# Four PSUM banks instead of three for the first MoE product, one of them freed by sharing; the first turn of keys in two instructions; one piece more per query unit

## The chip, the cores and the metric

The kernel runs on one core of a Trainium2 chip. The metric is the device time of one execution in microseconds. The engines are named as in the profile: PE is TensorE, DVE is VectorE, ACT is ScalarE, POOL is GpSimd, SP is SyncE, which here only issues DMAs. PEld is PE's loading of weights.

## The reference

Polysketch attention (4 batches, 4 heads, 1088 tokens, head dimension 32, sketch rank 8) is followed by a mixture of four experts with soft gates.

```python
a = einsum('rd,bhsd->bhsr', S1, x);  b = einsum('rd,bhsd->bhsr', S2, x)
phi(x) = outer(a, b) per token                       # 64 features
kv = einsum('bhsf,bhsd->bhfd', phi(k), v);  z = phi(k).sum(s)
attn = (phi(q) @ kv) / (phi(q) @ z + 1e-6)           # (B,H,S,D)
x = attn.transpose(0, 2, 1, 3).reshape(4352, 128)
p = domain_probs / (domain_probs.sum(-1) + 1e-9)     # (4352, 4)
out = sum_e p[:, e] * (relu(x @ w1[e]) @ w2[e])      # w1[e]: 128x1024, w2[e]: 1024x128
```

All is float32.

## The kernel before, in words

**The MoE is the backbone.** The 4352 tokens are cut into eleven chunks (`CHUNKS`: 128, 448, 512 six times, 320, 256, 128 columns). A chunk takes sixteen steps, one for each 256 of the 4096 hidden units. `first(i)` (line 744) makes two h tiles: for each it takes a PSUM bank with `psum(ps_h, "h")`, PE multiplies w1 by the transposed attention output `xT` into it, ACT writes the rectified half to `hid` (line 784), and DVE makes the sums and differences that a Strassen-like scheme wants (line 755). `second(i)` (line 798) is the product with w2, of seven block products instead of eight, which adds up in the two banks o0 and o1 over four steps. It runs for the step two earlier (`LA = 2`). At the end of an expert ACT copies o0 and o1 out (lines 889, 890) and POOL combines them (`gather`, `gather_rest`).

**Attention is cut into pieces.** The generator `front()` yields pieces of the next batch's keys and of the next query units; a unit is 128 to 512 tokens. `work()` is called after each h tile, so twice in a step, and calls `piece()` as often as a planner's credit allows. The planner adds up how many pieces must be done before each chunk can start (`needed`: 17 pieces for a batch's keys, 19 for a query unit, 21 for the first one), and spreads them evenly. A bare `yield` is an empty piece: it does no work and moves what follows to a later h tile. In each half step the program's order is: the h tile, then DVE's work on it, then the pieces. Every engine keeps its own part of this order.

**Keys** (`keys(b)`, line 423): three pieces turn the keys on DVE (`key_turn`, line 317; tiles 0 to 3, 4 to 7 and the last half tile), three project them on PE by the sketch matrix (`key_project_wide`, 4, 4 and 1 token tiles). ACT copies half of each projection from PSUM to SBUF (line 370), and DVE adds the other half to it (`key_add`, line 377). The add for group 0 is issued in the piece that projects group 1. Eight pieces form the 64 products by token and feature on DVE (`kp`, line 382), two pieces sum them against the values on PE (`key_sum`, into a bank of tag f), and one masks the result (`key_blocks`).

**Query units** (`queries`, line 608): turn the queries on DVE, project them on PE into f, shuffle and add on DVE, and form four products `qp` on DVE (line 485). After two empty yields comes `attend` (line 527): PE multiplies `qp` by the key sums into the bank `den` (three token tiles in a bank; a fourth goes to `num`), and DVE divides, turns and sends the result through DRAM into `xT`.

**PSUM** has eight banks of 512 float32 columns: three of tag h, o0, o1, f, den and num. A tag's bank is reused in turn, and the tile framework makes the new writer wait for the old tile's last reader.

**The start** (`start()`, line 653) does batch 0's keys and its first 128 queries at once, because PE has nothing else to do before the first `xT`: DVE turns keys (line 319) as soon as they land, PE projects them into three h banks and the queries into o0, o1 and num, DVE and POOL form products, PE sums them, and `attend_first` divides into `xT`. Three bf16 matmuls of zeros (`keep_warm`) run while PE waits.

Of the kernel before, what the change touches and what calls it, by code (L numbers as in the profile page):

```python
# [16 lines left out]
def _ap(t, p0: int, np_: int, off: int, free):  # L17

    p = list(t.ap)[0]
    return bass.AP(t.tensor, t.offset + p0 * p[0] + off, [[p[0], np_]] + [list(d) for d in free])  # L20
# [3 lines left out]
def kernel(  # L24
# [25 lines left out]
    P = 128  # L50
    HP = 64
    B, H, S, D = q.shape
# [20 lines left out]
    lpool = ctx.enter_context(tc.tile_pool(name="loads", bufs=1))  # L73
    apool = ctx.enter_context(tc.tile_pool(name="attn", bufs=1))
    mpool = ctx.enter_context(tc.tile_pool(name="moe", bufs=2))
    ps_h = ctx.enter_context(tc.tile_pool(name="ps_h", bufs=3, space=bass.MemoryType.PSUM))
    ps_o = ctx.enter_context(tc.tile_pool(name="ps_o", bufs=1, space=bass.MemoryType.PSUM))
    ps_f = ctx.enter_context(tc.tile_pool(name="ps_f", bufs=1, space=bass.MemoryType.PSUM))
    ps_n = ctx.enter_context(tc.tile_pool(name="ps_n", bufs=1, space=bass.MemoryType.PSUM))
# [3 lines left out]
    def psum(pool, tag):  # L83
        return pool.tile([P, 512], F32, tag=tag, name=tag)
# [25 lines left out]
    kn, qn, vn = {}, {}, {}  # L110
# [50 lines left out]
    kT = cpool.tile([P, P * NT], F32, name="kT")  # L161
# [152 lines left out]
    FG = ((0, 4), (4, 4), (8, 1))  # L314
    fss, kps, kvzs, kvx = {}, {}, {}, {}

    def key_turn(b, r):
        if r < 2:
            nc.vector.transpose(
                _ap(kT, 0, P, 512 * r, [[P, 4], [32, 4], [1, 32]]),  # L320
                _ap(kn[b], 0, P, P * r, [[32, 4], [8 * D, 4], [1, 32]]),
            )
        else:
            nc.vector.transpose(kT[:, 1024:S], kn[b][:, 1024:S])
# [98 lines left out]
    def keys(b):  # L423
        for r in range(3):
            key_turn(b, r)
            yield
        kf = []
        for gi, (pool, tag) in enumerate(((ps_f, "f"), (ps_n, "den"), (ps_n, "num"))):
            kf.append(psum(pool, tag))
            key_project_wide(b, gi, kf[gi])  # L430
            if gi:
                key_add(b, gi - 1, kf[gi - 1])
            yield
        for _ in value_copy(b):
            pass
        for t0, n in ((0, 4), (4, 5)):
            if t0:
                key_add(b, 2, kf[2])
            for p in range(2):
                for x in range(2):  # L440
                    key_product(b, t0, n, p, x, nc.vector)
                    yield
        kv = psum(ps_f, "f")
        for p in range(2):
            key_sum(b, p, kv)
            yield
        key_blocks(b, kv)
        yield
# [42 lines left out]

    def attend_first(b, c, n, qp):

        nd = [psum(ps_n, "den"), psum(ps_n, "num")]
        for _ in range(2):
            on_side(
                lambda s: nd[0][half[s], 0:n],
                lambda s: _ap(vx, 0, P, D, [[0, HP]]),
                lambda s: _ap(eps, 0, P, 0, [[0, n]]),
                start=True,  # L500
                stop=False,
            )
        for i in range(2):
            for _ in range(2):
                on_side(
                    lambda s: nd[i][half[s], 0:n],
                    lambda s: kvzs[b][:, s, 1 - i, :],
                    lambda s: qp[s][:, 0:n],
                    start=(i > 0),
                    stop=True,  # L510
                )
        yield

        rc = apool.tile([P, 2, HP], F32, tag="rd", name="rd")
        for i in range(2):
            by_g = [[32, 4], [1, 16]]
            nc.vector.reciprocal(_ap(rc, 0, P, HP * i, [[16, 4], [1, 16]]), _ap(nd[0], 0, P, 16 * i, by_g))  # L517
            nc.vector.tensor_tensor(
                out=_ap(xT, 0, P, HP * i, [[1, 4], [4, 16]]),
                in0=_ap(nd[1], 0, P, 16 * i, by_g),  # L520
                in1=_ap(rc, 0, P, HP * i, [[16, 4], [1, 16]]),
                op=ALU.mult,
            )
        have[0] += n
        yield

    def attend(b, c, n, qp):

        nd = [psum(ps_n, "den"), psum(ps_n, "num")]
        W = H * (D + 1)
        tiles = 0
        laid = []
        for c0, m in unit_parts(b, c, n):
            T = blocks(m)
            for p in range(2):
                for t in range(T[0]):
                    for _ in range(2):  # L540

                        at = c0 + P * t + (HP * turn[0] if t < T[turn[0]] else 0)
                        i, k = divmod(tiles + t, 3)
                        on_side(
                            lambda s: nd[i][half[s], W * k + W // 2 * p : W * k + W // 2 * (p + 1)],
                            lambda s: qp[p][:, at : at + HP],
                            lambda s: kvx[b][:, p, :],
                            start=True,
                            stop=True,
                        )  # L550
            laid.append((c0, T, tiles))
            tiles += T[0]
        yield
        banks = [(i, 3 * i, min(tiles, 3 * i + 3)) for i in range((tiles + 2) // 3)]
        rc = apool.tile([P, QW // 32], F32, tag="rc", name="rc")
        for i, t0, t1 in banks:
            nc.vector.tensor_scalar(
                out=rc[:, H * t0 : H * t1],
                in0=_ap(nd[i], 0, P, D, [[D + 1, H * (t1 - t0)]]),
                scalar1=1e-6, scalar2=1.0, op0=ALU.add, op1=ALU.mult,  # L560
            )
        nc.vector.reciprocal(rc[:, 0 : H * tiles], rc[:, 0 : H * tiles])
        yield
        xs = apool.tile([P, QW], F32, tag="qa", name="xs")
        for i, t0, t1 in banks:
            nc.vector.tensor_tensor(
                out=_ap(xs, 0, P, P * t0, [[D, H * (t1 - t0)], [1, D]]),
                in0=_ap(nd[i], 0, P, 0, [[D + 1, H * (t1 - t0)], [1, D]]),
                in1=_ap(rc, 0, P, H * t0, [[1, H * (t1 - t0)], [0, D]]),
                op=ALU.mult,  # L570
            )
        yield
        y = apool.tile([P, QW], F32, tag="y", name="y")
        for c0, T, t0 in laid:
            nc.vector.transpose(
                _ap(y, 0, P, P * t0, [[32, T[0]], [32 * T[0], H], [1, 32]]),
                _ap(xs, 0, P, P * t0, [[P, T[0]], [D, H], [1, D]]),
            )
            if b == 0 and c == P:
                for x in range(2):  # L580
                    yield
                    for a in (x, x + 2):
                        run = 32 * T[a // 2]
                        for h in range(H):
                            copy = nc.scalar.copy if h % 2 else nc.gpsimd.tensor_copy
                            at = S * b + c + a // 2 * 64 * T[0] + a % 2 * run
                            copy(xT[32 * h : 32 * h + 32, at : at + run], _ap(y, 32 * a, 32, 32 * T[0] * h, [[1, run]]))
                continue
            m = 64 * sum(T)
            base = xd.offset + P * (S * b + c + c0)  # L590
            for a in range(4):
                run = 32 * T[a // 2]
                nc.sync.dma_start(
                    bass.AP(
                        xd.tensor,
                        base + a // 2 * 64 * T[0] + a % 2 * run,
                        [[m, 32], [32 * m, H], [1, run]],
                    ),
                    _ap(y, 32 * a, 32, P * t0, [[32 * T[0], H], [1, run]]),
                )  # L600
            nc.sync.dma_start(
                xT[:, S * b + c + c0 : S * b + c + c0 + m],
                bass.AP(xd.tensor, base, [[m, P], [1, m]]),
            )
        have[0] += n
        yield

    def queries(b, c, n):
# [22 lines left out]
                yield  # L631
        yield
        yield
        yield from attend(b, c, n, qp)


# [16 lines left out]
    def start():  # L653
# [1 line left out]

        b, n = 0, UNITS[0][0]
        kf = []
        for r in range(3):
            key_turn(b, r)
        qT = query_turn(b, 0, n)  # L660
        for gi in range(3):
# [5 lines left out]
        key_project(b, 2, kf[2])  # L667
        for _ in value:
            pass
        fq = [psum(ps_o, "o0"), psum(ps_o, "o1"), psum(ps_n, "num")]  # L670
        for i in range(3):
            for j in range(2):
                both(fq[i][:, 0:n], sr[:, i, j, :], qT[:, 0:n], start=(j == 0), stop=(j == 1))
# [259 lines left out]
    for b in range(B):  # L933
        count += 17 if b else 0
        for n in UNITS[b] if b else UNITS[0][1:]:
            count, columns = count + (19 if count else 21), columns + n
            for m in range(NC):
                if columns - n < START[m] + CHUNKS[m] <= columns:
                    needed[m] = count
# [73 lines left out]
```

## Time and profile before

| | |
|---|---|
| median of 4 runs | 489.74 us (489.64 to 490.47) |
| the profiled execution | 489.55 us, of which the trace spans 487.6 us |
| PE busy | 481.7 us (99% of the span), 4545 matmuls |
| DVE busy | 323.5 us (66%) |
| ACT busy | 246.7 us (51%) |
| POOL busy | 228.3 us (47%) |
| granted TensorE clock | 1.0 |
| first MoE matmul | 13.58 us after the start of the span |

Times inside the trace count from the start of the span. A line of the groups gives the source line, engine and operation, the tiles out<-in, the shape and the number of instructions, then busy time and the mean of one in ns, and behind the second bar the engine's idle time just before them and what ended it. A PE row is a whole matmul with its latency, and several run at once, so PE's rate is read from the distance between starts. A float32 matmul shows as two rows. Line 193 is the helper that issues nearly all of them, so tile names tell them apart.

### The profile page before, as it was taken

Reading aid. Unit: us, or ns where it says so; the run is one execution under the profiler, and the core shown is the slowest. Engines: PE = TensorE matmul, PEld = TensorE weight load, DVE = VectorE, ACT = ScalarE, POOL = GpSimd, SP = SyncE. Lnnn points to the kernel's source line nnn. Section 1 sums busy time; section 2 is a strip of 40 time slices with the busy share of each in tenths; the row PEclk is TensorE's granted clock in tenths of the full one; section 3 lists DMA queues with packets and bytes.
Section 4 is the critical chain, followed back from the end, with each engine's and each line's share of the span. In section 5 each row is a group of like instructions: output and inputs, shape, how many; then the busy total and the mean of one; then the engine's idle time right before and its main releaser. Section 6 shows DMA issues by size and latency. Waiting matters only on the chain.

```text
span 487.6 us, 11352 instructions
## 1 busy us (share of the span) xinstructions
PE 481.7 (99%) x4545; PEld 359.7 (74%) x4545; DVE 323.5 (66%) x754; ACT 246.7 (51%) x496; POOL 228.3 (47%) x269
## 2 busy tenths in 40 slices
PE   8999999999999999999999999999999999999997
PEld 5877777677777777555777777777777777878997
DVE  6858685868776857768675676575575566655642
ACT  4364554445454635445455554545455455566751
POOL 6072563516345445324555353434555345555570
PEclk9999999999999999999999999999999999999999
DMA  7990230130103510041102200021101200120000
GB/s 209 290 301 6 85 98 1 32 107 1 35 1 109 126 40 1 1 118 24 34 1 86 50 2 2 1 86 24 34 0 56 50 1 0 50 51 3 15 3 18
DMA packets 37590, 26.25 MB, mean 54 GB/s; under 512 B 26018, under 2 KB 34594, under 8 KB 37026
## 3 DMA queue, kind: packets, MB, share of 16 engines
q1 hardware_dynamic: 37520, 25.53, 18.9%
q8 instruction: 36, 0.59, 0.5%
q14 instruction: 18, 0.13, 0.1%
q10 hardware_dynamic: 16, 0.00, 0.0%
HBM read 21.28 MB, written 4.24 MB: 52 GB/s over the span
## 4 chain that ended last, share of the span: by engine, by line
PE 96%; DVE 2%; issue 0%; DMA 0%; POOL 0%; ACT 0%; DVEq 0%
PE h L193 49%; PE o L193 40%; PE f L193 4%; PE den L193 2%; DVE qp L485 1%; DVE hid L755 1%; DMA s_raw<-in_S_dram 0%; PE num L193 0%; POOL sr L248 0%; ACT hid L784 0%; DVE qa L627 0%; DVE rd L517 0%; ACT sh L903 0%; POOL sp L243 0%; POOL sk L241 0%
## 5 line engine op out<-in xcount | busy, mean ns | idle before, releaser
L193 PE MATMUL h<-xT,w_sb 128*64 128x512 f32 (+5 forms) x1432 | 300.1, 490 | 0.1
L755 DVE SCALAR_TENSOR_TENSOR hid<-h,hid 128x256 f32<-128x256 f32 (+6 forms) x432 | 203.7, 472 | 141.8 <-ACT hid L784 133.4
L784 ACT ACTIVATE hid<-h 128x512 f32<-128x512 f32 (+3 forms) x288 | 158.5, 550 | 193.9 <-PE h L193 155.3
L193 PE MATMUL o<-hid,w2s 128*64 128x256 f32 (+3 forms) x1152 | 221.9, 355 | 0.0
L193 PE MATMUL o<-hid,w_sb 128*64 128x256 f32 (+3 forms) x864 | 183.6, 355 | 0.0
L193 PEld LDWEIGHTS h<-xT,w_sb 128*64 128x64 f32 x1432 | 143.6, 137 | 51.8 <-issue 10.8
L193 PEld LDWEIGHTS o<-hid,w2s 128*64 128x64 f32 x1152 | 132.7, 137 | 29.5 <-issue 0.2
L899 POOL TENSOR_TENSOR ev<-yz,sh 64x256 f32<-64x256 f32 (+3 forms) x72 | 48.0, 666 | 163.3 <-ACT sh L902 160.6
L193 PEld LDWEIGHTS o<-hid,w_sb 128*64 128x64 f32 x864 | 101.5, 137 | 25.9 <-issue 7.9
L887 POOL TENSOR_TENSOR yz<-ev 128x512 f32<-128x512 f32 (+3 forms) x36 | 42.0, 1168 | 58.2 <-ACT ev L890 58.1
L899 POOL TENSOR_TENSOR ct<-ev 128x512 f32<-128x512 f32 (+3 forms) x36 | 42.0, 1166 | 2.8
L485 DVE TENSOR_TENSOR qp<-qa,qb 64x384 f32<-64x384 f32 (+3 forms) x44 | 33.4, 758 | 1.1
L899 POOL TENSOR_TENSOR ct<-ct,gate 128x512 f32<-128x512 f32 (+3 forms) x27 | 32.2, 1194 | 2.1
L899 POOL TENSOR_TENSOR total<-total,ct 128x512 f32<-128x512 f32 (+3 forms) x27 | 31.7, 1175 | 2.1
L889 ACT COPY ev<-o 128x512 f32<-128x512 f32 (+3 forms) x36 | 19.4, 539 | 11.3 <-PE o L193 10.8
L193 PE MATMUL o<-w_sb,hid 128*64 128x128 f32 x256 | 21.6, 273 | 0.0
L890 ACT COPY ev<-o 128x512 f32<-128x512 f32 (+3 forms) x36 | 19.4, 540 | 2.4
L193 PEld LDWEIGHTS o<-w_sb,hid 128*64 128x64 f32 x256 | 17.7, 137 | 1.7 <-issue 1.5
L776 ACT ACTIVATE hid<-h 128x256 f32<-128x256 f32 x24 | 8.9, 384 | 18.9 <-PE h L193 18.4
L382 DVE TENSOR_TENSOR kp<-fs 128x256 f32<-128x256 f32 (+1 forms) x24 | 16.4, 684 | 0.1
L193 PEld LDWEIGHTS den<-kvx,qp 128*64 128x64 f32 x264 | 12.6, 137 | 3.3 <-issue 1.1
L902 ACT COPY sh<-yz 64x256 f32<-64x256 f32 (+3 forms) x36 | 13.7, 379 | 1.6 <-POOL yz L887 0.8
(122 smaller groups left out, 238.1 us busy)
## 6 DMA issues: line engine op xcount, KB each, us to landing
w_sb<-in_moe_w_dram SPq DMA_DIRECT2D x8, 512.0 KB, 7.7
gate<-gates SPq DMA_DIRECT2D x4, 1024.0 KB, 5.0
kn<-in_k_dram SPq DMA_DIRECT2D x4, 544.0 KB, 4.2
vn<-in_v_dram SPq DMA_DIRECT2D x16, 128.0 KB, 4.2
gate<-gates SPq DMA_DIRECT2D x2, 896.0 KB, 4.1
qn<-in_q_dram SPq DMA_DIRECT2D x3, 544.0 KB, 5.5
xd<-y SPq DMA_DIRECT2D x26, 48.0 KB, 1.7
out_dram<-ob SPq DMA_DIRECT2D x16, 64.0 KB, 2.0
```

The costliest lines, as they stand in the source:

```text
L193: nc.tensor.matmul(out(s), weights(s), moving(s), **flags)
L382: eng.tensor_tensor(out=_ap(kps[b], 0, P, 256 * t0 + P * p + 64 * x, [[256, n], [32, 2], [R, 4], [1, R]]), in0=_ap(src, 0, P, off + 4 * x, ...
L485: nc.vector.tensor_tensor(out=qp[p][64 * x : 64 * x + 64, 0:n], in0=qa[64 * p : 64 * p + 64, 0:n], in1=qb[64 * p : 64 * p + 64, 0:n], op=A ...
L755: nc.vector.scalar_tensor_tensor(out=out, in0=src, scalar=0.0, in1=in1, op0=ALU.max, op1=ALU.subtract)
L776: nc.scalar.activation(hd[:, 0 : 2 * n], hp[:, 0 : 2 * n], ACTF.Relu)
L784: nc.scalar.activation(hd[:, n * j : n * j + n], hp[:, 0:n], ACTF.Relu)
L887: add = lambda out, in0, in1, op=ALU.add: nc.gpsimd.tensor_tensor(out=out, in0=in0, in1=in1, op=op)
L889: nc.scalar.copy(_ap(ev, 0, P, 0, [[2 * w, 2], [1, w]]), _ap(a0, 0, P, 0, two))
L890: nc.scalar.copy(_ap(ev, 0, P, w, [[2 * w, 2], [1, w]]), _ap(a1, 0, P, 0, two))
L899: add = lambda out, in0, in1, op=ALU.add: nc.gpsimd.tensor_tensor(out=out, in0=in0, in1=in1, op=op)
L902: nc.scalar.copy(sh[HP:P, 0:w], yz[0:HP, 0, 0:w])
```

## The change

- `ps_h` gets a fourth bank. The tag num is gone; its four users take other banks: the third key projection takes f (the first one's bank), the second bank of `attend` takes f, that of `attend_first` takes o0, and the third query projection of the start takes an h bank.
- In `start()` the first turn of keys (tiles 0 to 3) is two DVE instructions of 256 columns instead of one of 512.
- A third empty yield stands between a query unit's products and `attend`; the planner counts 20 (22) pieces instead of 19 (21) for a unit.

```diff
-    ps_h = ctx.enter_context(tc.tile_pool(name="ps_h", bufs=3, space=bass.MemoryType.PSUM))
+    ps_h = ctx.enter_context(tc.tile_pool(name="ps_h", bufs=4, space=bass.MemoryType.PSUM))
...
-    def key_turn(b, r):
+    def key_turn(b, r, t0=0, n=4):
         if r < 2:
             nc.vector.transpose(
-                _ap(kT, 0, P, 512 * r, [[P, 4], [32, 4], [1, 32]]),
-                _ap(kn[b], 0, P, P * r, [[32, 4], [8 * D, 4], [1, 32]]),
+                _ap(kT, 0, P, 512 * r + P * t0, [[P, n], [32, 4], [1, 32]]),
+                _ap(kn[b], 0, P, P * r + 32 * t0, [[32, n], [8 * D, 4], [1, 32]]),
             )
...
-        for gi, (pool, tag) in enumerate(((ps_f, "f"), (ps_n, "den"), (ps_n, "num"))):
+        for gi, (pool, tag) in enumerate(((ps_f, "f"), (ps_n, "den"), (ps_f, "f"))):
...
     def attend_first(b, c, n, qp):
-        nd = [psum(ps_n, "den"), psum(ps_n, "num")]
+        nd = [psum(ps_n, "den"), psum(ps_o, "o0")]
...
     def attend(b, c, n, qp):
-        nd = [psum(ps_n, "den"), psum(ps_n, "num")]
+        nd = [psum(ps_n, "den"), psum(ps_f, "f")]
...
         yield
         yield
+        yield
         yield from attend(b, c, n, qp)
...
-        for r in range(3):
+        for t0 in (0, 2):
+            key_turn(b, 0, t0, 2)
+        for r in (1, 2):
             key_turn(b, r)
...
-        fq = [psum(ps_o, "o0"), psum(ps_o, "o1"), psum(ps_n, "num")]
+        fq = [psum(ps_o, "o0"), psum(ps_o, "o1"), psum(ps_h, "h")]
...
-            count, columns = count + (19 if count else 21), columns + n
+            count, columns = count + (20 if count else 22), columns + n
```

## The prediction, made before the changed kernel ran

> **What bounds the kernel now.** I read the busy shares first, then who PE waits for, then the places of those waits in the timeline.
>
> The page gives each engine's busy time, share of the span and instructions:
>
> ```profile
> PE 481.7 (99%) x4545; PEld 359.7 (74%) x4545; DVE 323.5 (66%) x754; ACT 246.7 (51%) x496; POOL 228.3 (47%) x269
> ```
>
> PE is the bound, so a change can win only where PE stands idle. The waits of PE (total, times, longest) are few:
>
> ```profile
> PE h L181 <- DVE s_hl L218: 1.2, 1, 1.2
> PE h L193 <- POOL sr L248: 0.6, 1, 0.6
> PE den L193 <- DVE qp L485: 0.4, 1, 0.4
> PE den L193 <- DVE kvz L405: 0.2, 1, 0.2
> ```
>
> Three of the four lie in the first 13 us; one, on `qp`, is in the body. None is for a bank of h: on PE's weight loads there are six waits on DVE's hid, 1.5 us in all, and none leaves PE's matmuls waiting. A 512-column step takes 3.23 us steadily, where 8x213 ns for h and 14x107 ns for o give 3.20 (these are the distances of starts).
>
> The start, in the timeline:
>
> ```profile
> 5.01 1.31 DVE L319 STREAM_TRANSPOSE kT<-kn 128x512 f32<-128x512 f32 x2 [0.98 <-DMA kn<-in_k_dram]
> ...
> 5.87 2.32 PE h L193 x72
> ```
>
> The profile names POOL's sr as the releaser of PE here, but in the built program PE waits for the copies of sk (over at 4.55) and for the first turn. That is two turns in 1.31 us, the first over at 5.72; PE follows 0.15 us later.
>
> The wait on `qp`:
>
> ```profile
> 197.19 1.65 DVE L485 TENSOR_TENSOR qp<-qa,qb 64x384 f32<-64x384 f32 x1
> ...
> 197.74 0.77 PE L193 MATMUL den<-kvx,qp 128*64 128x66 f32 x12
> ...
> 198.89 0.57 PE L193 MATMUL den<-kvx,qp 128*64 128x66 f32 x12 [0.38 <-DVE qp L485]
> ```
>
> This product took 1.65 us instead of the group's 0.84, because POOL began one at 197.14. The second dozen could have started at 197.74 + 0.77 - 0.22 (one row's latency) + 0.03 = 198.32; it started at 198.89: 0.57 lost.
>
> **What the Trainium skill says.** "SBUF — State Buffer", section "Who interferes with whom": a DVE instruction with two SBUF inputs and a GpSimd instruction that reads SBUF exclude each other, and the later one blocks. The trace agrees: `kp` and `qp`, with two SBUF inputs, reach 1606 and 1648 ns, while `key_add`, with one input in PSUM, keeps to 413 to 417 ns in all six large ones. "PSUM — Partial Sum Buffer", section "Specifications (TRN2)": eight banks per partition. So a fourth h bank must come from somewhere, and the skill's rule to guard by bank is the framework's wait that I cost below. "TensorE: Matmul & The Clock Gate", section "The mechanism": matmuls start and end strictly in order. Here too, so a waiting matmul holds all of PE.
>
> **The change part by part**, against the profiled 489.55 us.
>
> *Fourth h bank.* PE's matmuls wait nowhere for h, so it removes 0 (bounds: 0 to 0.2 us, the few steps that are some 0.05 us longer). It adds no instruction. If DVE fell further behind, it would be cover.
>
> *First turn in two.* 512 columns take 0.71 us here, 128 columns (qT) 0.27; on the line between, 256 take about 0.41. PE is released 0.30 us earlier. It needs 16 rows of 0.029 us for the first two tiles, 0.47 us, and the second half turn ends 0.34 us after the first, so PE doesn't wait again; the later turns come some 0.05 us later and are met too. DVE then had 0.83 us idle before its products, so the extra instruction is free. The 0.30 pass down: ACT's copy (7.06), products, the sum, `kvz` (DVE idle 0.44 before it), the divisions, and `xT` at 13.48, after which PE starts h at 13.58. But h also needs w1, whose load was issued at 7.40 and took 5.9 us to land: 13.30. With SP's queue unchanged, h can't start before about 13.37. So the gain is 13.58 - 13.37 = **-0.2** (bounds 0 and -0.3: a landing 0.2 later takes it all). The third projection in h and `attend_first` in o0 add no wait: qb's copy freed o0 at 9.87, and it is written at 12.33.
>
> *One more yield.* The order of the changed program puts the last product of this unit one half step ahead, in front of two hid instructions: about 195.2 instead of 197.19, ended by 196 even at 0.8 us, so clear of POOL's 197.14. PE wants it at 198.3. **-0.55** (bounds 0, if another collision takes 1.6 us there, and -0.7). In no unit is the distance from product to `den` below three half steps any more; before it was two in two units. 11 pieces more raise the planner's rate by a twentieth: the order of SP's DMAs and of POOL doesn't change, and results go out at most a half step later (about 1.6 us) where chunk 5's columns landed at 240.75 and were wanted at 244.6. The tightest, chunk 3's, keep their place.
>
> *num shared with f.* Here waits are added. The third key projection now writes the bank that `key_add` 0 reads. PE queues behind it: h, o, everything.
>
> Batch 1: the planner's new rate puts projections 1 and 2 in one half step (before: 0 and 1). Before, in this place (rows: start, duration, engine, line, instruction; idle time before it and its releaser in brackets):
>
> ```profile
> 58.66 0.95 PE L193 MATMUL h<-xT,w_sb 128*64 128x448 f32 x4
> 58.91 0.54 ACT L890 COPY ev<-o 128x448 f32<-128x448 f32 x1
> ...
> 59.41 0.42 PE L193 MATMUL num<-sk,kT 128*64 128x128 f32 x4
> ...
> 59.52 1.14 POOL L887 TENSOR_TENSOR yz<-ev 128x448 f32<-128x448 f32 x1 [2.92 <-ACT ev L890]
> 59.62 0.95 PE L193 MATMUL h<-xT,w_sb 128*64 128x448 f32 x4
> 59.69 0.54 ACT L784 ACTIVATE hid<-h 128x448 f32<-128x448 f32 x1 [0.25 <-ACT ev L890]
> ...
> 60.13 0.21 ACT L370 COPY fs<-num 128x64 f32<-128x64 f32 x1
> 60.27 0.39 DVE L755 SCALAR_TENSOR_TENSOR hid<-h,hid 128x224 f32<-128x224 f32 x1 [2.34 <-ACT hid L784]
> ```
>
> After: the 16 rows of projection 1 (0.87 us) move behind this h tile, so h starts at 57.79, and projection 2 is ready at 59.41 as before. `key_add` 0 stands on DVE behind this tile's hid: 60.27 - 0.87 = 59.40, and an add at that place ended 0.72 us after its hid started (60.27 to 60.99): 60.12. With 0.055 us to PE (as from kvz, 12.007 to 12.062): 60.17. **+0.76** (bounds 0.5 and 1.0).
>
> Batch 2: `key_add` 0 ended at 157.74, the projection came at 158.45: +0.
>
> Batch 3: the same three half steps as before. The add starts at 277.64 and takes 0.42: 278.06, plus 0.055; PE wanted the bank at 277.89: **+0.22** (0.1 to 0.4).
>
> *Sums of batch 1.* Both `key_sum` pieces now fall in one half step. The second starts at 71.99, when the first's 36 rows end, and not at 72.74. Its ninth pair of rows reads the last `kp`, at 71.99 + 16x0.029 = 72.46; that product ran from 72.16 for 0.48 to 72.64, plus 0.055: **+0.24** (bounds 0 and 1.4, by whether POOL collides with it).
>
> *f as `attend`'s second bank* is used by two units only, and free several pieces earlier: 0.
>
> Sum: -0.2 - 0.55 + 0.76 + 0.22 + 0.24 = +0.47. The profiled run would be 490.02. The median of the runs lies 0.19 above the profiled one, so I forecast 489.74 + 0.47 = **490.2 us**.
>
> **The rivals.** *The waits on f are covered* (chance 0.2): DVE reaches `key_add` sooner than I think, and only the gains stay: 489.74 - 0.75 = 489.0. For it: two of three batches are close to meeting the bank. Against: the add can't run before hid, hid not before ACT's rectifier, and that not before the h tile just ahead of the projection. *A collision on the last `kp` of batch 1* (0.15) ends slower: the second sum has lost its cover of one h tile, 0.75 us. POOL's yz ran there from 71.05 to 72.29. If a POOL instruction starts just ahead of the product, it takes 1.6 us as at 290.50, 1.12 more than 0.48. It decides as soon as the overlap is over about 0.5 us. 490.2 + 1.1 = 491.3. *The extra yield doesn't do what it says* (0.05): the product collides elsewhere and `den` waits as before: 490.2 + 0.55 = 490.75.
>
> **How the numbers follow.** My forecast has 0.6; its own range is 489.8 to 490.8 by the bounds of its two largest terms. To hold 8 in 10 I reach down to 489.0 and up to 490.9, leaving out the collision and part of the covered case. A measurement of this kernel tells about 0.2% (0.98 us) from no change, so the limits are 488.76 and 490.72. Below lies only the covered case with a full gain at the start: 0.07. Above lie the collision (0.15) and some of the rest: 0.18. Between: 0.75.
>
> **What would show it.** Right: PE's idle list holds two new entries before f, about 0.76 and 0.22 us, released by DVE's fs (line 377); den no longer waits on qp; the first h<-xT is near 13.37. Wrong: h before 13.3; no wait at the third projection; new waits of h on DVE; a long `kp` under a waiting f<-vx,kp.

## The result

The changed kernel takes 490.55 us (median of 34 runs, 489.94 to 491.35), the kernel before 489.75 (52 runs taken beside them). The ratio is 1.0016, with a 95% interval from 1.0011 to 1.0021: 0.8 us slower, where +0.47 was forecast (490.2). The difference is real by its interval, and lies within the 0.2% named ahead as no change. The profiled execution took 490.38 us with a span of 488.5.

PE is still the bound, with as many instructions as before. The busy times on the page of the changed kernel:

```profile
PE 482.2 (99%) x4545; PEld 368.1 (75%) x4545; DVE 319.5 (65%) x755; ACT 247.0 (51%) x496; POOL 228.9 (47%) x269
```

PE's waits in the changed kernel (engine and tile, whom it waits for: total, times, longest):

```profile
PE h L181 <- DVE s_hl L218: 1.2, 1, 1.2
PE f L193 <- DVE fs L377: 0.7, 1, 0.7
PE h L193 <- DMA w_sb<-in_moe_w_dram: 0.6, 1, 0.6
PE den L193 <- DVE kvz L405: 0.2, 1, 0.2
PE h L193 <- DVE kT L319: 0.2, 1, 0.2
```

The wait of den on qp is gone, as forecast, and a wait of f on fs (line 377, key_add) has come, as forecast. The wait of h on a weight load is new and was not forecast in this size. The wait of h on kT is the key projection of the start, which writes a bank of tag h; in the list before, the profile put the wait at this place to POOL's sr. The list ends at 0.2 us, so smaller losses must be found by setting both traces side by side. I took the start of every MoE step (the first h<-xT of a chunk and a pair of f) in both, and wrote down where the difference "after minus before" changes:

| place | forecast | difference added | running difference |
|---|---|---|---|
| first h, 13.8 us | -0.2 | +0.24 | +0.24 |
| four steps on, 17.3 us | | -0.14 | +0.10 |
| third key projection, batch 1, 60.4 us | +0.76 | +0.88 | +0.98 |
| key sums, batch 1, 73.7 us | +0.24 | +0.26 | +1.24 |
| up to chunk 4 | | +0.06 | +1.30 |
| products and den, chunk 4, 199 us | -0.55 | -0.77 | +0.53 |
| key projections, batch 3, 279 us | +0.22 | +0.32 | +0.85 |
| to the end | | 0.00 | +0.85 |

The two profiled executions differ by 490.38 - 489.55 = 0.83, the medians by 0.80: the table holds all of it.

*Batch 1.* The timeline of the changed kernel (start, duration, engine, line, instruction; idle time before it and its releaser in brackets):

```profile
57.88 0.95 PE L193 MATMUL h<-xT,w_sb 128*64 128x448 f32 x4
...
58.64 1.07 PE L193 MATMUL den<-sk,kT 128*64 128x128 f32 x16
...
58.92 0.55 ACT L787 ACTIVATE hid<-h 128x448 f32<-128x448 f32 x1 [0.25 <-ACT ev L893]
59.50 0.39 DVE L758 SCALAR_TENSOR_TENSOR hid<-h,hid 128x224 f32<-128x224 f32 x1 [1.79 <-ACT hid L787]
...
59.81 0.41 DVE L377 TENSOR_TENSOR fs<-f,fs 128x256 f32<-128x256 f32 x1
...
60.37 0.44 PE L193 MATMUL f<-sk,kT 128*64 128x128 f32 x4 [0.66 <-DVE fs L377]
...
60.61 0.95 PE L193 MATMUL h<-xT,w_sb 128*64 128x448 f32 x4
```

Read it upwards from the third projection (60.37): it waits for key_add 0 (59.81 to 60.22), which stands on DVE behind this tile's hid (59.50), which follows ACT's rectifier (58.92), which follows the h tile at 57.88. PE had room for only one projection (58.64, 16 rows) in that time. It is the bank that it waits for and not its data: all three turns of keys stand ahead of the first projection.

*Batch 3*, the same pattern in small. In the kernel before, PE wrote num while key_add 0 still ran:

```profile
277.64 0.42 DVE L377 TENSOR_TENSOR fs<-f,fs 128x256 f32<-128x256 f32 x1
...
277.89 0.38 PE L193 MATMUL num<-sk,kT 128*64 128x128 f32 x2
```

In the changed kernel hid comes at 277.82, key_add 0 behind it, and f behind that:

```profile
277.82 0.43 DVE L758 SCALAR_TENSOR_TENSOR hid<-h,hid 128x256 f32<-128x256 f32 x1 [2.18 <-ACT hid L787]
...
278.17 0.41 DVE L377 TENSOR_TENSOR fs<-f,fs 128x256 f32<-128x256 f32 x1
...
278.73 0.44 PE L193 MATMUL f<-sk,kT 128*64 128x128 f32 x4
```

Everything here runs 0.53 later than before. With this taken off, the add ends at 278.05, and f starts 0.15 behind it, at 278.20 instead of 277.89: 0.30 of the 0.32 in the table.

*Sums of batch 1.* In the kernel before an h tile stood between the two sums, and the last product had 0.58 us from its start to that of the second sum:

```profile
70.94 1.25 PE L193 MATMUL f<-vx,kp 128*64 128x66 f32 x36
...
71.98 0.95 PE L193 MATMUL h<-xT,w_sb 128*64 128x448 f32 x4
...
72.16 0.48 DVE L382 TENSOR_TENSOR kp<-fs 128x320 f32<-128x320 f32 x1
...
72.74 1.25 PE L193 MATMUL f<-vx,kp 128*64 128x66 f32 x36
```

Now they follow each other without it:

```profile
72.30 2.11 PE L193 MATMUL f<-vx,kp 128*64 128x66 f32 x58
...
73.14 0.48 DVE L382 TENSOR_TENSOR kp<-fs 128x320 f32<-128x320 f32 x1
```

The last product ends at 73.62. Row by row, the starts of f go 73.410, 73.433, 73.491, then 73.674, 0.055 after that end. POOL's instruction (72.03 to 73.26) overlapped this product by 0.12 only, and it took 0.48 as before. So the collision that was the rival ending slower did not take place.

*den and qp in chunk 4*:

```profile
197.32 0.42 DVE L758 SCALAR_TENSOR_TENSOR hid<-h,hid 128x256 f32<-128x256 f32 x1
197.77 0.55 DVE L485 TENSOR_TENSOR qp<-qa,qb 64x384 f32<-64x384 f32 x1
...
198.44 1.28 POOL L890 TENSOR_TENSOR yz<-ev 128x512 f32<-128x512 f32 x1 [1.57 <-ACT ev L893]
...
199.04 0.94 PE L193 MATMUL den<-kvx,qp 128*64 128x66 f32 x21
```

The last product takes 0.55 instead of 1.65 us and ends 0.72 us ahead of den; no bracket stands behind den. It ends only 0.12 us ahead of POOL's instruction.

*The start*:

```profile
4.96 1.36 DVE L319 STREAM_TRANSPOSE kT<-kn 128x256 f32<-128x256 f32 x3 [0.93 <-DMA kn<-in_k_dram]
...
5.55 2.32 PE L193 MATMUL h<-sk,kT 128*64 128x64 f32 x72 [0.22 <-DVE kT L319]
...
7.38 0.43 SPq L124 DMA_DIRECT2D w_sb<-in_moe_w_dram  x1
...
13.82 1.00 PE L193 MATMUL h<-xT,w_sb 128*64 128x64 f32 x27 [0.60 <-DMA w_sb<-in_moe_w_dram]
```

The key projection starts 0.32 us earlier (5.55 for 5.87; 0.05 of it because the first turn itself began earlier, at 4.96 for 5.01), and the chain keeps that as far as xT, whose first half is ready at 13.16 for 13.48. But w1, issued at the same time as before, landed 6.3 us later instead of 5.9, at about 13.7, and h waited for it.

### The profile page after: what moved, and what is told of

It reads as the page before. It is cut to its first block, busy times and chain, and to the rows that moved or that the text cites. A ratio compares the mean times of both kernels' runs of the same rounds, so it can differ in the third digit from the quotient of the medians.

```text
span 488.5 us, 11348 instructions
## 1 busy us (share of the span) xinstructions
PE 482.2 (99%) x4545; PEld 368.1 (75%) x4545; DVE 319.5 (65%) x755; ACT 247.0 (51%) x496; POOL 228.9 (47%) x269
## 4 chain that ended last, share of the span: by engine, by line
PE 96%; DMA 2%; SPq 1%; DVE 0%; issue 0%; ACT 0%
PE h L193 50%; PE o L193 41%; PE f L193 4%; PE den L193 2%; DMA w_sb<-in_moe_w_dram 1%; DMA kn<-in_k_dram 1%; SPq L147 0%; SPq L93 0%; ACT hid L787 0%; SPq L140 0%; SPq L119 0%; DVE hid L758 0%; DVE end L826 0%; DVE fs L377 0%
## 5 line engine op out<-in xcount | busy, mean ns | idle before, releaser
L193 PEld LDWEIGHTS h<-xT,w_sb 128*64 128x64 f32 x1432 | 147.7, 137 | 49.8 <-issue 9.5
L485 DVE TENSOR_TENSOR qp<-qa,qb 64x384 f32<-64x384 f32 (+3 forms) x44 | 29.3, 667 | 1.1
L905 ACT COPY sh<-yz 64x256 f32<-64x256 f32 (+3 forms) x36 | 13.7, 379 | 1.7 <-POOL yz L890 0.8
```

The lines of the kernel that those rows point to most:

```text
L193: nc.tensor.matmul(out(s), weights(s), moving(s), **flags)
L485: nc.vector.tensor_tensor(out=qp[p][64 * x : 64 * x + 64, 0:n], in0=qa[64 * p : 64 * p + 64, 0:n], in1=qb[64 * p : 64 * p + 64, 0:n], op=A ...
L905: nc.scalar.copy(sh[HP:P, 0:w], yz[0:HP, 0, 0:w])
```

## The experiments

Theory: the time is the sum of separate places where PE stands idle, each with its own cause (bank f behind key_add 0, sums in one half step, qp beside POOL, w1's landing). Rivals: the waits hang together, so that taking one away only moves it; or the start and its loads decide more than the body. All ratios are against the kernel before, run beside them on the same chip (489.62 to 489.87).

**1. key_add 0 issued in its own projection's piece** (changed kernel, one line):

```diff
-            if gi:
-                key_add(b, gi - 1, kf[gi - 1])
+            if gi != 1:
+                key_add(b, gi // 2, kf[gi // 2])
```

> The changed kernel with one instruction of DVE issued earlier: key_add of group 0 stands in the piece of its own projection, not in that of the next one, so it no longer queues behind another tile's hid. Theory (the shared bank f is a wait on DVE's key_add 0, and its place in DVE's order makes it late): PE's waits for f at the third key projection of batches 1 and 3 (0.88 and 0.21 us in the two traces) go, and the time falls by 0.9 to 1.1 us, from 490.55 to about 489.5. Rival (the bank is late because of ACT's fs copy, or DVE gets stuck earlier and hid comes late instead): the time stays at 490.4 to 490.6, and new waits for hid or o stand in place of those for f.

Measured: 489.45 us, ratio 0.9992 (0.9984 to 1.0000). The same place in its timeline:

```profile
57.83 0.41 DVE L377 TENSOR_TENSOR fs<-f,fs 128x256 f32<-128x256 f32 x1
...
58.85 1.07 PE L193 MATMUL den<-sk,kT 128*64 128x128 f32 x16
...
59.71 0.39 DVE L758 SCALAR_TENSOR_TENSOR hid<-h,hid 128x224 f32<-128x224 f32 x1 [1.46 <-ACT hid L787]
59.72 0.42 PE L193 MATMUL f<-sk,kT 128*64 128x128 f32 x4
```

The same instruction now runs two microseconds earlier, before the h tile, and the third projection follows the second without a gap. Step by step the difference to the changed kernel is -0.88 in batch 1 and -0.32 in batch 3, so all that the two places had cost. No new wait of PE stands in the list; near 133 us 0.18 is lost in small parts, whose cause stays open. The cost of the shared bank is the place of one DVE instruction in DVE's order; the rival (ACT's copy, or hid late instead) falls.

**2. Two yields and the old counts** (changed kernel):

```diff
         yield
         yield
-        yield
         yield from attend(b, c, n, qp)
...
-            count, columns = count + (20 if count else 22), columns + n
+            count, columns = count + (19 if count else 21), columns + n
```

> The changed kernel with two empty yields before attend instead of three and the planner's old counts 19 and 21; the banks and the split turn stay. Theory (the extra piece buys the qp wait and pays with crowded half steps in batch 1): the wait of den on qp near 198 us is back (+0.77), the lost 0.88 at the third projection of batch 1 and the 0.26 at its sums are gone, batch 3's 0.21 stays: 490.55 + 0.77 - 0.88 - 0.26 = about 490.2. Rival (the shared bank costs batch 1 the same whatever the piece's place): 490.55 + 0.77 - 0.26 = 491.05.

Measured: 490.22 us, ratio 1.0008 (1.0000 to 1.0016); forecast 490.2. Its timeline shows the product beside POOL and the wait of den back, and in batch 1 a third projection that waits for nothing, though it writes the same shared bank:

```profile
57.69 0.41 DVE L377 TENSOR_TENSOR fs<-f,fs 128x256 f32<-128x256 f32 x1
...
59.58 0.42 PE L193 MATMUL f<-sk,kT 128*64 128x128 f32 x4
...
197.36 1.64 DVE L485 TENSOR_TENSOR qp<-qa,qb 64x384 f32<-64x384 f32 x1
...
199.06 0.57 PE L193 MATMUL den<-kvx,qp 128*64 128x66 f32 x12 [0.37 <-DVE qp L485]
```

Step by step against the changed kernel: -0.88 and -0.25 in batch 1, +0.76 at den, and batch 3 as there. So the 0.88 needs both edits: the shared bank alone costs batch 1 nothing.

**3. The yield alone** (kernel before, third yield and counts 20 and 22; diff as in the change).

> The kernel before with only the third yield and the planner's counts 20 and 22; three banks of h, num kept apart. Theory: the qp wait goes (-0.77), the two sums of batch 1 fall into one half step (+0.26), no projection waits: 489.75 - 0.5 = about 489.25. Rival (the gain at qp is a matter of the whole changed kernel's timing): the product meets another POOL instruction and the time stays at 489.7 to 490.0.

Measured: 489.37 us, ratio 0.9992 (0.9984 to 1.0000). Step by step: +0.26 at the sums, -0.77 at den, nothing at a projection. With the second experiment this makes a square of four kernels: wait at batch 1's projection in one of them only, that with the yield and the shared bank.

**4. Three banks of h** (changed kernel; the eighth bank serves the third query projection of the start and nothing else):

```diff
-    ps_h = ctx.enter_context(tc.tile_pool(name="ps_h", bufs=4, space=bass.MemoryType.PSUM))
+    ps_h = ctx.enter_context(tc.tile_pool(name="ps_h", bufs=3, space=bass.MemoryType.PSUM))
...
-        fq = [psum(ps_o, "o0"), psum(ps_o, "o1"), psum(ps_h, "h")]
+        fq = [psum(ps_o, "o0"), psum(ps_o, "o1"), psum(ps_n, "num")]
```

> The changed kernel with three banks of h instead of four; the eighth bank is used once, at the start, for the third query projection. Everything else as changed. Theory (PE's matmuls never wait for a bank of h, so the fourth bank is worth nothing): 490.55 within 0.15 and the same waits. Rival (the fourth bank hides part of the delays of DVE that the shared f brings): 0.3 to 0.8 us slower, with waits of h on hid.

Measured: 490.54 us, ratio 1.0014 (1.0008 to 1.0021), and from the first h to the last step the starts agree with the changed kernel's to 0.02 us. The fourth bank of h, for which the others were moved together, brings nothing.

**5. The split turn alone** (kernel before with the two short turns).

> The kernel before with only the first turn of keys in two instructions. Theory (the chain of the start gains 0.3 us and then meets the landing of the first w1 load, which is no earlier): the first key projection starts at 5.55, the first h no earlier than 13.3, and the time is between 489.55 and 489.85, depending on when the load lands. Rival (the start is set by the chain through xT alone): 489.75 - 0.3 = 489.45.

Measured: 489.77 us, ratio 0.9998 (0.9990 to 1.0006). The gain is not seen. In its timeline h waits for w1, which landed 6.1 us after its issue:

```profile
5.69 2.47 PE L193 MATMUL h<-sk,kT 128*64 128x64 f32 x72
...
13.73 1.06 PE L193 MATMUL h<-xT,w_sb 128*64 128x64 f32 x29 [0.27 <-DMA w_sb<-in_moe_w_dram]
```

**6 and 7. The first w1 load ahead of the rest of q**, in the kernel before (6) and in the changed one (7):

```diff
+    load_w1(0)
     load_rows(q, 0, "qn", slice(P, S))
     for e in range(E):
-        load_w1(e)
+        if e:
+            load_w1(e)
         load_w2(e)
```

> The kernel before with the first w1 load issued ahead of the rest of q, one place earlier on SP's queue. Theory (in the kernel before w1 lands at 13.30, 0.28 us ahead of the first h, so an earlier landing is worth nothing): 489.75 within 0.15. Rival (in part of the runs w1 lands later than xT is ready, and this makes their spread): 0.1 to 0.3 us faster, and a narrower spread than the 489.35 to 490.47 seen.

> The changed kernel with the first w1 load issued ahead of the rest of q. Theory (the split turn's gain of 0.32 is cancelled by the wait of the first h for w1): the first h moves from 13.82 to about 13.25, the 0.6 us wait for w1 is gone, and the time falls by 0.3 to 0.5, to about 490.15. Rival (DMA traffic decides, and the rest of q comes late instead): the wait moves to the first query turn and the time stays at 490.4 to 490.7.

Measured: 489.66 us, ratio 1.0000 (0.9992 to 1.0009), and 490.18 us, ratio 1.0012 (1.0005 to 1.0018). So the earlier load is worth nothing without the split. With it, the distance to the kernel before beside it falls from 0.80 to 0.56, so it would be worth 0.2, but the intervals overlap. (The 13 runs of 6 lie within 0.67 us and the 53 of the kernel before within 1.06; such unlike numbers of runs don't settle whether late loads make the spread.) w1 now lands 3.8 to 3.9 us after its issue, near 10.7, and no h waits for it. Yet in the profiled execution of 7 the first h starts at 13.95 and not at the 13.25 expected. The reason is in the key projection, and it was new to me. In the timeline of the changed kernel with w1 early:

```profile
5.70 2.88 PE L195 MATMUL h<-sk,kT 128*64 128x64 f32 x72
```

The same 72 rows took 2.32 us in the changed kernel's own profile, shown above. The difference of 0.56 and a first turn 0.15 later make up the 0.7 us. Over all executions with ten matmuls on zeros ahead, these rows take 2.3 us in some and 2.5 to 2.9 in others. Between row starts, a pair of rows goes from 0.107 us to 0.058 at some moment: PE begins at half its rate. The profile's row of granted clock reads full speed in all these slices, so it doesn't show this. The Trainium skill does tell of it ("TensorE: Matmul & The Clock Gate", section "What's actually happening"): PE starts at half clock and is let go after about 3.4 us of work, by a free-running window, so that the moment differs from run to run. The traces agree in the main: PE's first matmul is at 1.19 in all of them, and the full rate comes between 4.7 and 6.95 us, so 3.5 to 5.8 us later. The page gives the variation as about 500 ns either way; here it is wider, 2.2 us from first to last.

| kernel | first turn of keys | full rate from | first h | step 4 |
|---|---|---|---|---|
| before | 5.01 | 4.7 | 13.58 | 17.20 |
| 9, no split, w1 early | 5.12 | 4.8 | 13.69 | 17.30 |
| 3, no split | 5.21 | 6.9 | 14.16 | 17.78 |
| changed | 4.96 | 4.9 | 13.82 (waits for w1) | 17.30 |
| 5, split alone | 5.10 | 6.1 | 13.73 (waits for w1) | 17.22 |
| 7, changed, w1 early | 5.11 | 6.95 | 13.95 | 17.61 |
| 8, split, w1 early | 5.04 | 6.9 | 13.94 | 17.55 |
| 11, changed and mended | 4.96 | 4.7 | 13.21 | 17.18 |

The first turn starts when kn has landed, and its difference passes down. Taken off, before and 9 agree (17.20 and 17.30 - 0.11 = 17.19), and 3 lies at 17.78 - 0.20 = 17.58: a late full rate costs about 0.4 us there, about a third of the spread between runs of one and the same kernel, 489.35 to 490.47. That it makes this spread is not shown: the profiled executions of 3, 7 and 8, with a late full rate, lie 0.40, 0.52 and 0.65 us above their kernels' medians, but that of 2, with the full rate from 6.6, lies 0.18 below its own.

**8 and 9. The gains without the costs**: the kernel before with third yield, w1 early, and one empty piece ahead of a batch's key sums, with the split turn (8) and without (9). num stays. What is new in the diff:

```diff
+        yield
         kv = psum(ps_f, "f")
         for p in range(2):
             key_sum(b, p, kv)
...
-        count += 17 if b else 0
+        count += 18 if b else 0
```

> The gains without the costs: the kernel before with the third yield, the split turn, the first w1 load ahead of the rest of q, and one empty piece more ahead of a batch's key sums (counts 18 for the keys, 20 and 22 for the units) so that the two sums of batch 1 lie in two half steps; three banks of h and num kept. Theory: qp wait gone (-0.77), start -0.3, sums +0: 489.75 - 1.07 = about 488.7. Rival (the extra pieces crowd another place or the start's gain is eaten by w1): 489.0 to 489.4.

> The version with the gains alone (third yield, first w1 load early, an empty piece ahead of the key sums, num kept), but with the first turn of keys in one instruction again. Theory (with w1 out of the way the split turn is worth 0.3 us where PE's rows of the start run at full rate, and about half of it where they begin at half rate): 488.71 + 0.15 to 0.3 = 488.85 to 489.0. Rival (the split is worth nothing even with w1 early): 488.7.

Measured: 488.71 us, ratio 0.9982 (0.9975 to 0.9989), and 489.18 us, ratio 0.9983 (0.9976 to 0.9989). Both beat both kernels. In the body, step by step, 8 gains 0.48 us on the kernel before: nothing at the sums of batch 1 (the empty piece gives them their h tile back), a loss of 0.37 in small parts up to chunk 3, and a gain of 0.85 at den. Of the waits of PE that the profile lists only two are left, both in the start:

```profile
PE h L183 <- DVE s_hl L220: 1.2, 1, 1.2
PE den L195 <- DVE kvz L407: 0.2, 1, 0.2
```

8 and 9 ran on different chips, where the kernel before took 489.62 and 489.87. Their distances to the kernel before beside them are 0.91 and 0.69 us, so the split would be worth 0.2 with w1 early, but the intervals overlap nearly whole. The table gives less. Brought to the turn at 5.01, the executions with a late full rate reach step 4 at 17.51 (7) and 17.52 (8) with the split and at 17.58 (3) without it; those with an early one at 17.23 (11) with it and at 17.20 and 17.19 (before, 9) without.

**10. Three instead of ten matmuls on zeros ahead of the first key projection** (kernel before, line 183; they compute nothing, and stand apart from the three in `start()`):

```diff
-    keep_warm(10)
+    keep_warm(3)
```

> The kernel before with 3 instead of 10 matmuls on zeros ahead of the first key projection (they compute nothing). Theory (the start, and the spread of a kernel's own runs, hang on when PE goes from half to full rate, seen in the traces between 4.7 and 6.9 us): PE is then at half rate through the whole key projection, 72 rows at 0.053 instead of 0.029 us, so the first h comes 1.5 to 3 us later: 491.2 to 492.7. Rival (the spread is that of the loads alone and the rate is no matter): 489.6 within 0.3.

Measured: 491.83 us, ratio 1.0038 (1.0025 to 1.0052). Its timeline:

```profile
1.19 1.46 PE L181 MATMUL h<-warm 128*128 128x512 bf16 x3 [1.19 <-DVE s_hl L218]
5.93 3.76 PE L193 MATMUL h<-sk,kT 128*64 128x64 f32 x72 [3.27 <-POOL sr L248]
...
15.10 1.19 PE L193 MATMUL h<-xT,w_sb 128*64 128x64 f32 x33
```

72 rows in 3.76 us instead of 2.32; the full rate comes at about 9.2, near the end of the projection. The first h is 1.52 later, step 4 is 2.42 later (0.87 of it an idle stretch of PE before 17.15 that the profile puts down to issue), and the medians differ by 2.0. PE's rate in the first microseconds does set the first h; what the idle stretch behind it has to do with the rate stays open.

**11. The changed kernel, mended**: key_add 0 moved as in 1, w1 early as in 7, the empty piece as in 8.

> The changed kernel with its three costs mended: key_add 0 issued in its own projection's piece, the first w1 load ahead of the rest of q, and one empty piece ahead of the key sums (count 18). Four banks of h, f shared. Theory (the terms add up): 490.55 - 0.88 - 0.21 - 0.37 - 0.26 = about 488.8. Rival (the mends meet one another, or the shared bank costs something the list of waits doesn't show): 489.1 to 489.5.

Measured: 488.87 us, ratio 0.9979 (0.9971 to 0.9987). The costs add up and can be taken away one by one: step by step, the difference to the changed kernel is -0.88 and -0.26 in batch 1 and -0.33 in batch 3. Beside experiment 8, which has num and three banks of h (0.91 below the kernel before, this one 1.00), the shared bank costs nothing more. Here the full rate came early, w1 was there, and the first h started at 13.21 as reckoned. Still, four steps on the gain of 0.37 on the kernel before was all but gone (17.18 for 17.20), 0.24 of it between f and the first o. In the timeline:

```profile
7.86 0.43 SPq L127 DMA_DIRECT2D w_sb<-in_moe_w_dram  x1
...
13.21 1.65 PE L195 MATMUL h<-xT,w_sb 128*64 128x64 f32 x48
...
14.44 0.94 ACT L782 ACTIVATE hid<-h 128x256 f32<-128x256 f32 x3 [4.89 <-PE h L195]
14.83 0.97 PE L195 MATMUL f<-qT,sq 128*64 128x448 f32 x4
15.84 0.66 PE L195 MATMUL o<-w_sb,hid 128*64 128x128 f32 x8
```

The first o could follow f at 15.61 and starts at 15.84. The list of waits of PE's weight loads names ACT's hid:

```profile
PEld o L195 <- ACT hid L782: 0.8, 1, 0.8
```

But the hid that it reads, the first of the three, was over at 14.82. Its other operand is w2, whose first load was issued at 7.86 and landed 7.8 us later, at about 15.7. So behind w1 the next load seems to be the limit. That w2 is the cause is read from these times; no run moved that load.

## Why the prediction came out as it did

The sign, the places and the mechanisms of the body were right. Point by point:

- *Fourth h bank, 0*: shown (experiment 4).
- *One more yield, -0.55*: shown (experiments 2 and 3). Time lost at den itself fell by 0.60; the other 0.17 of the -0.77 shows from 204 us on with no wait of PE listed, and its cause stays open. My place for the product was wrong: I had it at 195.2 on the old scale, where the third product had stood, but that one moved by 0.4 only (196.10 - 1.30 = 194.80) and a hid still stands between, so the last came at 197.77 - 1.30 = 196.47. Its margin to POOL is 0.12 us and not 1.1: the gain came nearer to the failing case than I said.
- *Third projection, batch 1, +0.76*: shown (experiments 1 to 3), measured +0.88. The chain h, rectifier, hid, key_add 0, projection is the one written down. The start of the h tile is at 57.88 - 0.10 = 57.78 on the old scale, as forecast (57.79). The add ended at 60.22 - 0.10 = 60.12, as forecast too. But the projection's rows started 0.15 behind the add's end (60.37 - 60.22) and not 0.055, a distance that I had taken from another pair of instructions.
- *Batch 2, 0*: no change in the table's differences there.
- *Batch 3, +0.22*: measured +0.32, and gone with the add's move (experiment 1). The add ended as forecast (278.05 for 278.06); what was short is the same distance from the add's end to the rows, 0.15 and not 0.055.
- *Sums of batch 1, +0.24*: +0.26, at the very row named, and gone with the empty piece (experiment 8).
- *First turn in two, -0.2*: this step failed. "With SP's queue unchanged, h can't start before about 13.37" took one landing of w1, 13.30, for a fixed time. Without the edit of the load, it lay 4.7 to 6.3 us behind its issue in eight executions, between 12.3 and 13.7. In the profiled one of the changed kernel it was late, and the term was +0.24 at the first h and +0.10 four steps on. The bound of 0 excluded a loss because the chain itself could only get shorter. Also, the start was read as one chain at one rate: PE's change of rate (4.7 to 6.95 us), w1 and then w2 each cut the gain. By experiment 5 the split alone is worth between -0.5 and +0.3 us.
- *The steady step, 3.20*: in the trace the starts of h rows lie 214.5 ns apart and those of o rows 108 (medians), not 213 and 107; with these the step comes to the measured 3.23. No term hangs on it.

By the table the sum of +0.47 missed +0.85 by the start (0.30), batch 1 with its sums (0.14), batch 3 (0.10) and the small changes up to chunk 4 (0.06), less the larger gain at den (0.22). That the total came this near is in part luck: 0.60 was missed one way, and a gain larger for reasons not foreseen gave 0.22 back.

## What to carry to other kernels

A bank shared by two users ties PE to the reader of the first one: what it costs is not in the number of banks but in where that reader stands in its engine's order, and here one instruction issued a piece earlier gave back 1.0 us (0.80 above the kernel before, then 0.22 below it). An edit that shifts a planner's rate moves every piece, so place each one anew, the neighbours of the piece aimed at as well, and look for two that now fall together. A gain in a kernel's first microseconds is limited by the next load and by PE's own rate; take landing times from several executions before counting on one.

## What the runs showed of the hardware

- PE begins at half rate and goes to full rate between 4.7 and 6.95 us in kernels whose first 4 us are the same; a pair of 64-column rows then takes 0.058 instead of 0.107 us. Seven matmuls on zeros fewer put it off to 9.2 us and cost 2.0 us, 1.5 of them at the first h. The column of granted clock showed nothing of it.
- The same load of 512 KB, issued at 7.4 to 7.6 us, landed 4.7 to 6.3 us later; issued one place earlier in the queue, ahead of 480 KB, it landed 3.8 to 3.9 us later in four executions and 5.9 in a fifth.
